# Attention and two feed-forward stages on one core: eight one-bank PSUM tiles in place of four two-bank tiles, and a new table of steps

## The chip, the core and the metric

The kernel runs on one core of a Trainium2 chip. The metric is the device time of one execution in microseconds (us). The engines are named as the profile names them: PE (TensorE, the matrix engine), PEld (its weight loads), DVE (VectorE), ACT (ScalarE), POOL (GpSimd) and SP (SyncE, which issues the DMAs here).

## What is computed

Causal attention over 2 x 12 heads of 448 tokens and 64 dimensions, whose output (896 tokens x 768) goes through two feed-forward stages. Only the attention is touched by the change.

```python
scores = scale * np.matmul(q, k.transpose(0, 1, 3, 2))
scores = np.where(mask, -1000000000.0, scores)
scores = scores - np.max(scores, axis=-1, keepdims=True)
attn = np.exp(scores)
attn = attn / (np.sum(attn, axis=-1, keepdims=True) + 1e-09)
x = np.matmul(attn, v)                      # heads laid side by side: 896 x 768
h = x @ w_in                                # 768 x 2048
x = (h * (1.0 / (1.0 + np.exp(-h)))) @ w_out
# then a second stage: 768 x 1024, softmax, product, layer norm, 1024 x 768
```

## The kernel before

The 24 heads are done as 12 pairs, two heads at a time on the two halves of the 128 partitions. A pair's 448 queries are cut into seven units u of 64 queries; unit u needs only the first 64(u+1) keys. For a pair p the steps are these, with the names that the table of steps uses:

- **Sa, Sb** (line 164): scores of units 6, 4, 2, 0 and of units 5, 3, 1, by PE into PSUM.
- **m p.u** (line 170): DVE reads a unit's scores out of PSUM, adds the mask, writes them to the buffer e in SBUF and leaves the row's extreme in st.
- **e p.u** (line 175): ACT takes the exponential in place and sums the row. **r p** (lines 180, 181): DVE adds 1e-9 to the seven sums and takes reciprocals.
- **n p.u** (line 188 on POOL, marked G in the table; line 186 on ACT, marked A): the unit is multiplied by its reciprocals.
- **T p.0, T p.1** (line 202): PE transposes the pair's 16 blocks of 64 queries x 128 keys, for each head, into PSUM, 16 instructions a step.
- **x p.0 to x p.3** (line 216 on ACT, line 214 on DVE, marked V): the transposed weights are copied to the SBUF buffer aT.
- **P p** (line 229): PE multiplies them with the values. **h p** (line 238) and **l p** (line 243) take the result out of PSUM as a rounded part and a rest.
- **g 0 to g 3**: four half blocks of nine matmuls each of the first feed-forward product (lines 395 to 397), put among the last pairs; the weights for them are converted by w, ca, sh (line 276), sl (line 264), rh (line 271), sp, wl, which DVE, ACT and POOL do beside the attention.

Nothing is scheduled by itself here: the text ORDER is read from left to right, and each engine's instructions stand in that order in its queue. An engine works its queue strictly in order, so a step that waits holds all that stands behind it on the same engine. The number after a slash names the PSUM slot that a step writes. Before, there are four slots of two banks each (`SLOTS = 4`). A slot is one tile, so a step that takes it over waits until everything in both banks has been read: T 4.1 into slot 3, which holds the scores Sa of pair 6, waits for the maxima of units 6, 4, 2 and 0 of pair 6. P takes a slot of two banks and fills one. The copies x p.0 to x p.3 are cut by key block, for both heads together, and are 896, 128, 640 and 384 columns wide.

The pieces that set this:

```python
def slot(n):
    return (pss if n == SLOTS - 1 else psx).tile([128, 2, 512], F32, name=f"x{n}", tag=f"x{n}")
PARTS_T = [[(0, range(UNITS)), (3, range(6, UNITS))], [(1, range(2, UNITS)), (2, range(4, UNITS))]]
```

Behind the attention follow only matmuls of the feed-forward stages on PE, with the conversion of weights, activations and evictions on the other engines. The attention and the four g steps end where the ninth matmul of g 3 gives way to the main loop of line 395.

## Time and profile before

| | us |
|---|---|
| median of 3 runs | 397.04 (396.93 to 397.53) |
| the profiled execution: its own time | 397.12 |
| the profiled execution: span of the core | 395.2 |
| PE busy in the span | 387.5 |
| DVE, ACT, POOL busy in the span | 290.3, 279.7, 188.6 |
| granted TensorE clock | 1.00 of full speed in all slices |

The span is the time from the first to the last instruction of the core; the 1.9 us between it and the execution's own time lie around it. Busy times overlap, since the engines work side by side. A row of the timeline gives the start, the length and the count of a run of equal instructions; a bracket at its end tells how long the engine stood idle before it and what ended that.

### The profile page before, as it was taken

What the parts mean: (1) busy time and instruction counts of PE and PEld (TensorE: products, weight loads), DVE (VectorE), ACT (ScalarE), POOL (GpSimd) and SP (SyncE); (2) the same over time, 40 slices, a digit from 0 to 9 for tenths busy, and PEclk for the clock granted to TensorE, in tenths of its full rate; (3) what the DMA queues carried; (4) which work ended last, traced back from release to release, by engine and by line L of the source; (5) the groups of instructions that cost most, each with busy time, mean ns of one, the idle gap of its engine ahead of it and who ended that gap; (6) DMA issues with size and microseconds to landing.
All of it is one profiled execution on the core that took longest, in us unless ns stands there. A gap on an engine that the chain in (4) does not pass through costs nothing.

```text
span 395.2 us, 8157 instructions
## 1 busy us (share of the span) xinstructions
PE 387.5 (98%) x2914; PEld 364.0 (92%) x2914; DVE 290.3 (73%) x681; ACT 279.7 (71%) x655; POOL 188.6 (48%) x236
## 2 busy tenths in 40 slices
...
GB/s 235 399 213 139 101 7 77 81 127 153 127 116 119 121 119 120 117 124 202 89 152 120 191 179 230 238 245 224 14 80 121 98 62 2 20 41 41 41 81 60
DMA packets 20152, 49.68 MB, mean 126 GB/s; under 512 B 2320, under 2 KB 4880, under 8 KB 20112
## 3 DMA queue, kind: packets, MB, share of 16 engines
...
q8 instruction: 23, 0.38, 0.4%
...
## 4 chain that ended last, share of the span: by engine, by line
PE 92%; DVE 4%; ACT 3%; issue 0%
PE h L397 8%; PE h L396 8%; PE h L395 8%; PE h L824 5%; PE h L825 5%; PE h L826 5%; PE ps L904 5%; PE h L555 4%; PE h L557 4%; PE h L556 4%; PE ps L906 4%; PE ps L905 4%; PE x L229 4%; PE x L164 3%; ACT e L175 3%; PE x L202 2%
## 5 line engine op out<-in xcount | busy, mean ns | idle before, releaser
L259 ACT ACTIVATE wr<-wr 128x384 f32<-128x384 f32 x92 | 54.3, 591 | 10.4 <-DMA wr<-w_in 10.2
L396 PE MATMUL h<-l,wh 128*128 128x448 f32 x174 | 61.3, 352 | 0.0
L395 PE MATMUL h<-h,wh 128*128 128x448 f32 x174 | 61.3, 352 | 0.0
L397 PE MATMUL h<-h,wl 128*128 128x448 f32 x174 | 61.3, 352 | 0.0
L289 DVE SCALAR_TENSOR_TENSOR pw<-wr,pw 128x384 uint32<-128x384 uint32 x78 | 43.5, 557 | 13.3 <-ACT pw L285 13.2
L188 POOL TENSOR_TENSOR e<-e,st 128x64 f32<-128x64 f32 (+6 forms) x76 | 45.5, 633 | 11.4 <-DVE st L170 6.9
L414 POOL TENSOR_TENSOR gl<-sg,gh 128x448 fp32r<-128x448 f32 x29 | 32.7, 1145 | 36.9 <-ACT sg L412 36.9
L175 ACT ACTIVATE e<-e,st 128x256 f32<-128x256 f32 (+6 forms) x84 | 41.8, 507 | 4.2 <-DVE st L170 4.1
L326 DVE TENSOR_TENSOR wl<-pw,wh 128x384 fp32r<-128x384 f32 x30 | 16.7, 557 | 32.5 <-ACT wh L322 31.8
L322 ACT ACTIVATE wh<-pw 128x384 fp32r<-128x384 f32 x30 | 14.8, 493 | 36.1 <-PE h L396 27.5
L170 DVE CUSTOM_DVE_ANT_0 e<-x,mask 128x448 f32<-128x448 f32 (+6 forms) x84 | 30.5, 414 | 5.4 <-PE x L164 5.4
L858 POOL TENSOR_TENSOR s<-s,mhalf 128x1 f32<-128x1 f32 x7 | 4.2, 594 | 61.3 <-DVE s L857 61.3
L326 POOL TENSOR_TENSOR wl<-wx,wh 128x384 fp32r<-128x384 f32 x21 | 21.2, 1008 | 25.5 <-ACT wh L322 25.4
L395 PEld LDWEIGHTS h<-h,wh 128*128 128x128 f32 x174 | 32.9, 189 | 0.1
L397 PEld LDWEIGHTS h<-h,wl 128*128 128x128 f32 x174 | 32.9, 189 | 0.0
L396 PEld LDWEIGHTS h<-l,wh 128*128 128x128 f32 x174 | 32.9, 189 | 0.0
L824 PE MATMUL h<-w3h,h 128*128 128x512 f32 x84 | 31.9, 380 | 0.0
L825 PE MATMUL h<-w3l,h 128*128 128x512 f32 x84 | 31.9, 379 | 0.0
L826 PE MATMUL h<-w3h,l 128*128 128x512 f32 x84 | 31.8, 379 | 0.0
L555 PE MATMUL h<-gh,wh 128*128 128x448 f32 x90 | 31.7, 352 | 0.0
L557 PE MATMUL h<-gh,wl 128*128 128x448 f32 x90 | 31.7, 352 | 0.0
L556 PE MATMUL h<-gl,wh 128*128 128x448 f32 x90 | 31.7, 352 | 0.0
...
## 6 DMA issues: line engine op xcount, KB each, us to landing
...
gain<-gl_in SPq DMA_DIRECT2D x1, 4.0 KB, 3.9
```

Of the source, the lines that this page charges most:

```text
L175: nc.scalar.activation(ep(p, u), ep(p, u), AF.Exp, bias=st[p % 4][:, u:u + 1], scale=-1.0, accum_out=st[p % 4][:, 8 + u:9 + u])
L188: eng.tensor_tensor(ep(p, u), ep(p, u), r.to_broadcast([128, wide(u)]), ALU.mult)
L259: nc.scalar.activation(high, high, AF.Copy, scale=DOWN)
L395: nc.tensor.matmul(ps[:, :S], wh, rh, start=turn == 0 and k % NB == 0, stop=False)
L396: nc.tensor.matmul(ps[:, :S], wh, rl, start=False, stop=False)
L397: nc.tensor.matmul(ps[:, :S], wl, rh, start=False, stop=turn == 1 and k % NB == NB - 1)
L555: nc.tensor.matmul(ps[:, :S], wh, rh, start=f == CF[0], stop=False)
L556: nc.tensor.matmul(ps[:, :S], wh, rl, start=False, stop=False)
L557: nc.tensor.matmul(ps[:, :S], wl, rh, start=False, stop=f == CF[-1])
L824: nc.tensor.matmul(ps[:, n], yh[k][:, at], wh, start=k == 0, stop=False)
L825: nc.tensor.matmul(ps[:, n], yh[k][:, at], wl, start=False, stop=False)
L826: nc.tensor.matmul(ps[:, n], yl[k][:, at], wh, start=False, stop=k == KD - 1)
```

## The change

PSUM is cut into eight tiles of one bank (`SLOTS = 8`, 512 columns). A step names one bank a digit: Sa and Sb take two, T takes two (one a head), P takes one. Each bank is given back when its own contents have been read. The transposed weights lie in aT by head and block (head, 16 blocks of 64 columns, key blocks in the order 0, 3, 1, 2), and the copies x p.0 to x p.3 become four equal ones of 512 columns: first and second half of the blocks, each for head 0 and head 1. The second product reads them at the places that `FROM_T` gives. No matmul and no maximum is added or taken away. The table of steps is new as a whole. Net of all, ACT has five instructions less and POOL five more: the norms 4.4, 8.0, 8.1, 10.4 and 10.1 and the conversion ca 3 go from ACT to POOL, in pair 11 ACT does four norms in place of three; h 11 goes from ACT to DVE; ACT does 25 of the 48 copies x in place of 24, DVE 23.

```diff
--- before.py
+++ after.py
@@ -48,7 +48,7 @@
 MASKED = -1.0e9 / SCALE
 
 
-SLOTS = 4
+SLOTS = 8
 UNITS = S // C
 SWAPPED = (1, 2, 3, 4)
 BANKS = ((6, 0), (4, 2), (5,), (3, 1))
@@ -59,27 +59,28 @@
 
 
 ORDER = """
-q1 q2 q3 v0 Sx0/0 v1 v2 m0.1 Sy0 m0.0 e0.1 e0.0 Sz0 m0.3 m0.2 e0.3 Sw0 m0.5 e0.2 e0.5 Sa1/3 m0.4 q4 m0.6 w0 e0.4 Sb1/1
...
+q1 q2 q3 v0 Sx0/0 v1 v2 m0.0 Sy0 m0.1 e0.1 e0.0 Sz0 m0.2 Sw0 m0.3 e0.2 m0.5 e0.3 e0.5 Sa1/45 m0.4 q4 m0.6 w0 e0.4
...
 """
 
 
@@ -147,7 +148,7 @@
         scs = {}
 
         def slot(n):
-            return (pss if n == SLOTS - 1 else psx).tile([128, 2, 512], F32, name=f"x{n}", tag=f"x{n}")
+            return (pss if n >= SLOTS - 2 else psx).tile([128, 512], F32, name=f"x{n}", tag=f"x{n}")
 
         sa, sb, sc = {}, {}, {}
 
@@ -156,7 +157,7 @@
             banks, swapped = (BANKS, SWAPPED) if p else (FIRST_BANKS, FIRST)
             for u in us:
                 n = next(n for n, bank in enumerate(banks) if u in bank)
-                t = (sa, sb, sc)[n // 2][p][:, n % 2]
+                t = (sa, sb, sc)[n // 2][p][n % 2]
                 o = sum(wide(v) for v in banks[n][:banks[n].index(u)])
                 scs[p, u] = t = t[:, o:o + wide(u)]
                 for j in range(2):
@@ -191,25 +192,23 @@
 
         aT, trs = {}, {}
 
-        PARTS_T = [[(0, range(UNITS)), (3, range(6, UNITS))], [(1, range(2, UNITS)), (2, range(4, UNITS))]]
-        HALVES = [[(u, kb) for kb, us in part for u in us] for part in PARTS_T]
+        BLOCKS_T = [(u, kb) for kb in (0, 3, 1, 2) for u in range(2 * kb, UNITS)]
+        FROM_T = [BLOCKS_T.index((2 * kb, kb)) for kb in range(NKB)]
 
         def transp(p, g, n):
-            t = slot(n).rearrange("k h (n q) -> k h n q", q=C)
-            for m, (u, kb) in enumerate(HALVES[g]):
+            for h in range(2):
+                trs[p, 2 * g + h] = slot(int(n[h]))
+            for m, (u, kb) in enumerate(BLOCKS_T[8 * g:8 * g + 8]):
                 for h in range(2):
-                    r = slice(C * h, C * h + C)
-                    nc.tensor.transpose(t[:, h, m], es[p % EB][r, AT[u] + kb], ident[r, r])
-            trs[p, g] = t
+                    r, t = slice(C * h, C * h + C), trs[p, 2 * g + h]
+                    nc.tensor.transpose(t[:, C * m:C * m + C], es[p % EB][r, AT[u] + kb], ident[r, r])
 
         def evict(p, n, eng):
             if p not in aT:
-                aT[p] = att.tile([128, NKB, 2, S], F32, name="aT", tag=f"aT{p % AB}", bufs=1)
-            a = aT[p]
-            kb, us = PARTS_T[n // 2][n % 2]
-            m = n % 2 and len(HALVES[n // 2]) - len(us)
-            src = trs[p, n // 2][:, :, m:m + len(us)]
-            dst = a[:, kb, :, C * us[0]:].rearrange("k h (n q) -> k h n q", q=C)
+                aT[p] = att.tile([128, 2, 16, C], F32, name="aT", tag=f"aT{p % AB}", bufs=1)
+            g, h = divmod(n, 2)
+            dst = aT[p][:, h, 8 * g:8 * g + 8]
+            src = trs[p, n].rearrange("k (n q) -> k n q", q=C)
             if eng is nc.vector:
                 eng.tensor_copy(dst, src)
             else:
@@ -218,15 +217,16 @@
         pvs = {}
 
         def pv(p, n):
-            t = pvs[p] = slot(n)[:, 0]
+            t = pvs[p] = slot(n)
             v = vs[p]
             for z in range(NKB):
                 for lo, hi, swap in RUNS if p else FIRST_RUNS:
-                    sl = slice(C * max(lo, 2 * z), C * hi)
+                    lo = max(lo, 2 * z)
+                    sl, at = slice(C * lo, C * hi), FROM_T[z] + lo - 2 * z
                     for h in range(2):
                         j = h ^ swap
                         if sl.start < sl.stop:
-                            nc.tensor.matmul(t[64 * j:64 * j + 64, sl], v[:, j, z], aT[p][:, z, h, sl],
+                            nc.tensor.matmul(t[64 * j:64 * j + 64, sl], v[:, j, z], aT[p][:, h, at:at + hi - lo],
                                              start=z == lo == 0, stop=z == NKB - 1, skip_group_check=True)
 
         def pv_hi(p, eng):
@@ -435,7 +435,7 @@
             rounded(th[4][:, k], tl[4][:, k], sgs[FB[k], 0], nc.gpsimd)
 
         nc.vector.memset(xl[0][:, :S].bitcast(F32), 0.0)
-        wp = slot(SLOTS - 1)[:, 0]
+        wp = slot(SLOTS - 1)
 
         def warm(count):
             for _ in range(count):
@@ -467,19 +467,19 @@
             gemm1(f, half, 0, turn)
 
         def scores_to(tiles, p, n, us):
-            if n is not None:
-                tiles[p] = slot(n)
+            if n:
+                tiles[p] = [slot(int(b)) for b in n]
             scores(p, us)
 
         emit = {
-            "Sx": lambda p, n, u, e: scores_to(sa, p, n, (0, 1)), "Sy": lambda p, n, u, e: scores_to(sb, p, 1, (2, 3)),
-            "Sz": lambda p, n, u, e: scores_to(sc, p, 2, (5,)), "Sw": lambda p, n, u, e: scores(p, (6, 4)),
+            "Sx": lambda p, n, u, e: scores_to(sa, p, "01", (0, 1)), "Sy": lambda p, n, u, e: scores_to(sb, p, "2", (2, 3)),
+            "Sz": lambda p, n, u, e: scores_to(sc, p, "4", (5,)), "Sw": lambda p, n, u, e: scores(p, (6, 4)),
             "Sa": lambda p, n, u, e: scores_to(sa, p, n, (6, 4, 2, 0)), "Sb": lambda p, n, u, e: scores_to(sb, p, n, (5, 3, 1)),
             "q": lambda p, n, u, e: load_pair(p), "v": lambda p, n, u, e: load_v(p),
             "w": lambda m, n, u, e: load_w(*order[m]),
             "m": lambda p, n, u, e: maxes(p, u), "e": lambda p, n, u, e: exps(p, u), "r": lambda p, n, u, e: recip(p),
             "n": lambda p, n, u, e: norm(p, u, e), "T": lambda p, n, u, e: transp(p, u, n),
-            "x": lambda p, n, u, e: evict(p, u, e), "P": lambda p, n, u, e: pv(p, n),
+            "x": lambda p, n, u, e: evict(p, u, e), "P": lambda p, n, u, e: pv(p, int(n)),
             "h": lambda p, n, u, e: pv_hi(p, e), "l": lambda p, n, u, e: pv_lo(p),
             "ca": lambda m, n, u, e: conv_a(1, m, e), "sh": lambda m, n, u, e: shift_w(1, m),
             "sl": lambda m, n, u, e: sign_low(1, m, fresh(xs)), "rh": lambda m, n, u, e: rest_high(1, m),
@@ -493,7 +493,7 @@
             step, _, part = step.rstrip("AVG").partition(".")
             name = step.rstrip("0123456789")
             u = int(part) if part else None
-            emit[name](int(step[len(name):]), int(n) if n else None, u, e)
+            emit[name](int(step[len(name):]), n, u, e)
         fed[0] = EARLY
         gm = gm[0]
         psx.release()
```

The first place is PE's queue at pair 2 (buffer e2; x with a digit is the PSUM slot or bank). Before, from the transposes T 2.0 on:

```order
L202 MATMUL x3_476<-ident_70,e2_99 128x64 x16
L164 MATMUL x1_496<-qk_211 64x448 x2
L164 MATMUL x1_496<-qk_211 64x320 x2
L164 MATMUL x1_496<-qk_211 64x192 x2
L164 MATMUL x1_496<-qk_211 64x64 x2
L202 MATMUL x2_514<-ident_70,e2_99 128x64 x16
L164 MATMUL x0_534<-qk_211 64x384 x2
L164 MATMUL x0_534<-qk_211 64x256 x2
L164 MATMUL x0_534<-qk_211 64x128 x2
L229 MATMUL x3_550<-aT_509,v32_159 64x64 x2
```

With the change, from the last two of the 32 transposes of the same pair on:

```order
L204 MATMUL x7_513<-ident_70,e2_99 128x64
L204 MATMUL x5_514<-ident_70,e2_99 128x64
L165 MATMUL x6_533<-qk_214 64x448 x2
L165 MATMUL x0_534<-qk_214 64x320 x2
L165 MATMUL x0_534<-qk_214 64x192 x2
L165 MATMUL x6_533<-qk_214 64x64 x2
L165 MATMUL x4_550<-qk_214 64x384 x2
L165 MATMUL x3_551<-qk_214 64x256 x2
L165 MATMUL x3_551<-qk_214 64x128 x2
L229 MATMUL x5_564<-aT_544,v32_160 64x64 x2
```

Both halves of the transposes now stand together ahead of all seven units of scores (of pair 5), where before scores stood between them.

The second place is DVE's queue ahead of the transposes of pair 4, with the maxima of pair 6 (buffer e2; x3 and x0 are slots before, x6, x7 and x0 banks now). Before, T 4.1 goes into slot 3 and needs all of x3_623 read:

```order
L271 SCALAR_TENSOR_TENSOR wx_505<-wr_196,wx_505 128x384
L214 COPY aT_619<-x1_601 128x2x192
L214 COPY aT_619<-x1_601 128x2x320
L170 ISA e2_99,st2_103<-x3_623,mask_96 128x448
L170 ISA e2_99,st2_103<-x0_636,mask_96 128x128
L170 ISA e2_99,st2_103<-x3_623,mask_96 128x320
L180 TENSOR_SCALAR st1_102<-st1_102 128x7
L181 RECIPROCAL st1_102<-st1_102 128x7
```

With the change T 4.1 goes into banks 4 and 6 and needs, of these, x6_653 alone:

```order
L213 COPY aT_638<-x1_619 128x512
L213 COPY aT_638<-x4_620 128x512
L271 SCALAR_TENSOR_TENSOR wx_510<-wr_198,wx_510 128x384
L171 ISA e2_99,st2_103<-x6_653,mask_96 128x64
L171 ISA e2_99,st2_103<-x6_653,mask_96 128x448
L171 ISA e2_99,st2_103<-x7_654,mask_96 128x320
L181 TENSOR_SCALAR st1_102<-st1_102 128x7
L182 RECIPROCAL st1_102<-st1_102 128x7
```

The two copies moved ahead of line 271, and the two maxima that T 4.1 waits for stand first; before, the last one that it waits for (128x192 of x3_623) stood behind the reciprocals and two further maxima.

The third place is ACT's queue at the copies of pairs 1 and 2 (aT_414 and aT_509 before; aT_425 and aT_544 now; e3 belongs to pair 3, e0 to pair 4, h1 is the taking-out of pair 1). Before:

```order
L216 ACTIVATE aT_414<-x0_374 128x896
L216 ACTIVATE aT_414<-x0_374 128x2x64
L175 ACTIVATE e3_100,st3_104<-e3_100,st3_104 128x192
L175 ACTIVATE e3_100,st3_104<-e3_100,st3_104 128x384
L175 ACTIVATE e3_100,st3_104<-e3_100,st3_104 128x128
L175 ACTIVATE e3_100,st3_104<-e3_100,st3_104 128x448
```

With the change:

```order
L215 ACTIVATE aT_425<-x1_384 128x512
L176 ACTIVATE e3_100,st3_104<-e3_100,st3_104 128x128
L176 ACTIVATE e3_100,st3_104<-e3_100,st3_104 128x448
L215 ACTIVATE aT_425<-x7_385 128x512
L176 ACTIVATE e3_100,st3_104<-e3_100,st3_104 128x384
L176 ACTIVATE e3_100,st3_104<-e3_100,st3_104 128x320
L176 ACTIVATE e0_97,st0_101<-e0_97,st0_101 128x192
L176 ACTIVATE e0_97,st0_101<-e0_97,st0_101 128x320
L176 ACTIVATE e0_97,st0_101<-e0_97,st0_101 128x128
L238 ACTIVATE h1_74<-x1_458 128x448
L176 ACTIVATE e0_97,st0_101<-e0_97,st0_101 128x64
L176 ACTIVATE e0_97,st0_101<-e0_97,st0_101 128x384
```

Two exponentials of pair 3 now stand between the two copies of pair 1; behind the last row follow the two copies of pair 2.

## Rows read from the trace of the kernel before

**Rows 1.** The page: busy time of each engine; the chain that ended last, by engine

```profile
PE 387.5 (98%) x2914; PEld 364.0 (92%) x2914; DVE 290.3 (73%) x681; ACT 279.7 (71%) x655; POOL 188.6 (48%) x236
...
PE 92%; DVE 4%; ACT 3%; issue 0%
```

**Rows 2.** Busy time by stretch: length, then PE, PEld, DVE, ACT, POOL

```profile
40.00:45.00 5.00, 5.00 (x98) 4.01 (x100) 4.85 (x21) 5.00 (x19) 4.49 (x10) 1.00 0.44 161
73.00:395.00 322.00, 318.45 (x1773) 308.88 (x1771) 228.15 (x440) 213.97 (x438) 133.09 (x126) 1.00 0.38 117
```

**Rows 3.** Timeline of PE, 14 to 36 us: start, length, what, idle before it

```profile
16.67 1.99 PE L229 MATMUL x<-aT,v 128*64 128x256 f32 x36 [0.79 <-ACT aT L216]
18.59 1.21 PE L202 MATMUL x<-ident,e 64*128 64x64 f32 x32
19.73 1.74 PE L164 MATMUL x<-qk 64*64 64x448 f32 x28
21.40 1.98 PE L229 MATMUL x<-aT,v 128*64 128x64 f32 x32
23.31 0.71 PE L202 MATMUL x<-ident,e 64*128 64x64 f32 x16
...
24.98 0.71 PE L202 MATMUL x<-ident,e 64*128 64x64 f32 x16
...
26.43 1.98 PE L229 MATMUL x<-aT,v 128*64 128x64 f32 x32
28.34 1.50 PE L202 MATMUL x<-ident,e 64*128 64x64 f32 x32
29.77 1.74 PE L164 MATMUL x<-qk 64*64 64x448 f32 x28
...
33.41 0.71 PE L202 MATMUL x<-ident,e 64*128 64x64 f32 x16
34.58 0.72 PE L202 MATMUL x<-ident,e 64*128 64x64 f32 x16 [0.46 <-DVE st L170]
35.22 1.09 PE L164 MATMUL x<-qk 64*64 64x448 f32 x12
```

**Rows 4.** The same timeline: the first matmul of g 3

```profile
72.48 0.46 PE L395 MATMUL ps<-h,wh 128*128 128x448 f32 x1
```

**Rows 5.** Timeline of DVE, 29 to 35 us

```profile
29.78 1.23 DVE L271 SCALAR_TENSOR_TENSOR wx<-wr,wx 128x384 uint32<-128x384 uint32 x1
...
32.13 0.61 DVE L170 CUSTOM_DVE_ANT_0 e<-x,mask 128x448 f32<-128x448 f32 x1
...
34.07 0.35 DVE L170 CUSTOM_DVE_ANT_0 e<-x,mask 128x192 f32<-128x192 f32 x1
```

**Rows 6.** Timeline of ACT, 19 to 22 us

```profile
19.57 1.07 ACT L216 ACTIVATE aT<-x 128x896 f32<-128x896 f32 x2
...
21.57 0.39 ACT L175 ACTIVATE e<-e,st 128x128 f32<-128x128 f32 x1
...
21.95 0.66 ACT L175 ACTIVATE e<-e,st 128x448 f32<-128x448 f32 x1
```

**Rows 7.** Groups by line and shape, 0 to 75 us: busy us, mean ns

```profile
L216 ACT ACTIVATE aT<-x 128x896 f32<-128x896 f32 x11 | 10.0, 912 | 0.0
L214 DVE COPY aT<-x 128x640 f32<-128x640 f32 x11 | 9.0, 817 | 0.0
...
L214 DVE COPY aT<-x 128x384 f32<-128x384 f32 x11 | 6.0, 547 | 0.0
...
L271 DVE SCALAR_TENSOR_TENSOR wx<-wr,wx 128x384 uint32<-128x384 uint32 x5 | 3.8, 762 | 0.0
...
L216 ACT ACTIVATE aT<-x 128x128 f32<-128x128 f32 x11 | 3.0, 272 | 1.0 <-PE x L202 1.0
```

**Rows 8.** The same view: norms on POOL, and the conversion ca

```profile
L188 POOL TENSOR_TENSOR e<-e,st 128x320 f32<-128x320 f32 x10 | 7.2, 719 | 0.9 <-DVE st L181 0.9
...
L188 POOL TENSOR_TENSOR e<-e,st 128x128 f32<-128x128 f32 x10 | 4.3, 430 | 0.4 <-DVE st L181 0.4
...
L257 POOL TENSOR_TENSOR wr<-wr,down 128x384 f32<-128x384 f32 x4 | 3.3, 827 | 0.0
```

More of the change, by code (lines that the diff above doesn't have):

```diff
@@ L67 @@
-x1.3V n2.4G e3.5 m4.6 n2.6G P1/0 e3.1 q8 m4.1 m4.4 e3.6 v7 n2.3G m4.2 e4.1 m4.0 r3 ca0G e4.2 m4.3 T2.0/3 e4.4 m4.5
-n3.2G Sa5/1 sl0 h1A n3.1G x2.1A n3.5G e4.0 l1 T2.1/2 x2.0A n3.0G m5.0 Sb5/0 m5.2 n3.4G e5.0 x2.2V e4.6 n3.3G q9 x2.3V
-P2/3 e4.3 n3.6G v8 m5.5 e4.5 m5.3 ca1G e5.5 m5.4 T3.0/2 r4 h2A ca2G m5.6 e5.4 l2 T3.1/1 n4.5G x3.1A x3.0A m5.1 Sa6/3
-rh0 n4.2G e5.6 n4.0G Sb6/0 x3.3V n4.1G n4.4A x3.2V n4.6G e5.1 P3/2 q10 e5.3 m6.6 n4.3G v9 e5.2 m6.1 m6.4 e6.1 r5 e6.4
-T4.0/1 m6.3 n5.5G h3A m6.0 m6.2 x4.0A m6.5 T4.1/3 n5.2G l3 n5.1G Sa7/0 x4.1A e6.2 n5.4G x4.2V e6.3 Sb7/1 n5.0G x4.3V
@@ L82 @@
-P10/2 rh3 x11.2A x11.3A w7 sp3 P11/1 h10A wl3 l10 g3 h11A l11
+q1 q2 q3 v0 Sx0/0 v1 v2 m0.0 Sy0 m0.1 e0.1 e0.0 Sz0 m0.2 Sw0 m0.3 e0.2 m0.5 e0.3 e0.5 Sa1/45 m0.4 q4 m0.6 w0 e0.4
+Sb1/67 v3 m1.4 e0.6 m1.6 q5 e1.4 Sa2/23 r0 w1 m1.2 e1.6 n0.4G v4 m1.5 Sb2/01 e1.2 m1.1 n0.2G m2.6 e1.1 q6 n0.5G Sb3/56
+e1.5 m1.0 m2.0 w2 m1.3 n0.3G Sa3/42 e1.0 v5 m2.1 m2.3 e2.0 n0.1G m2.4 e1.3 n0.0G m3.2 q7 n0.6G e2.3 r1 w3 e2.4 m3.4 v6
+n1.4G m2.2 T0.0/71 e2.1 m3.6 e2.2 T0.1/23 n1.5G m2.5 x0.1A x0.3V n1.0G x0.0A n1.1G e2.5 x0.2V n1.3G P0/0 e2.6 m3.3
@@ new lines @@
+n1.6G m3.5 e3.3 r2 n1.2G e3.2 m3.1 m3.0 n2.4G T1.0/17 h0A sh0 e3.0 T1.1/32 n2.1G l0 x1.0A n2.5G Sa4/56 e3.1 x1.3V e3.6
+n2.2G x1.2V Sb4/40 n2.0G x1.1A ca0G m4.6 e3.5 q8 P1/1 m4.3 n2.3G v7 m4.2 e3.4 m4.0 n2.6G m4.4 e4.2 m4.1 e4.4 r3 m4.5
+T2.1/23 n3.3G e4.1 sl0 h1A T2.0/75 n3.6G e4.0 Sa5/60 e4.5 x2.3V n3.1G x2.1A x2.2V n3.0G Sb5/43 n3.5G x2.0A m5.0 l1
+e5.0 n3.4G P2/5 q9 e4.3 m5.5 v8 ca1G e4.6 m5.1 m5.4 m5.3 e5.1 n3.2G m5.2 e5.3 ca2G r4 T3.0/27 h2A m5.6 T3.1/14 n4.1G
+x3.1A l2 n4.5G Sb6/30 x3.0A x3.2V e5.6 Sa6/67 n4.6G x3.3V e5.2 rh0 P3/5 n4.4G e5.4 q10 e5.5 v9 n4.3G m6.0 m6.6 n4.0G
```

27 lines of the change are left out of this document (13 added, 14 removed).

## The prediction

> **What bounds the kernel now.** I read the page first: PE is busy 98% of the span and holds 92% of the chain that ended last [rows 1]. The stretches split this. From 73 us on PE has work 318.45 of 322 us, while DVE, ACT and POOL have idle time; no part of that stretch is touched by the change. So a microsecond by which the attention ends sooner or later on PE should reach the end almost whole. In the attention three further engines are close to full: from 40 to 45 us ACT is busy 5.00 of 5, DVE 4.85, POOL 4.49 [rows 2]. There PE leads by little, and a queue that is reordered can push it in either direction.
>
> The timeline of PE shows what is to be had. An undisturbed pair is the one that starts at 18.59: transposes to 19.73 (1.14), scores to 21.40 (1.67), values to 23.31 (1.91), together 4.72 us [rows 3]. The attention ends with g 3 starting at 72.48 [rows 4]. Whatever PE loses against the undisturbed pair between 16.67 and 72.48 is the change's to gain; matmuls themselves are the same before and after, so none of them gets shorter.
>
> **The change part by part.**
>
> *Copies.* ACT did one copy of 896 columns (912 ns) and one of 128 (272), together 1184; DVE did 640 (817) and 384 (547), together 1364 [rows 7]. A line through ACT's two gives 592 for 512 columns, through DVE's two 682: twice that is 1184 and 1364. Cost and gain nil. The layout of aT moves the same columns; I put nothing for it, since PE reads runs of the same lengths.
>
> *Start.* PE begins the first product with the values at 16.67, released by ACT's copy [rows 3]. In ACT's queue 19 exponentials stand ahead of that copy in both kernels, the same pieces of pairs 0 to 2, and then two copies of equal sum. I put no gain; a gain can't be over the 0.79 us of that wait.
>
> *Pair 2 of the transposes.* Scores stand between its halves. From 23.31 to the values at 26.43 PE takes 3.12 us; the undisturbed pair does the same work in 2.81 (18.59 to 21.40) [rows 3]. The new table keeps the halves together: **-0.31**.
>
> *Pair 3.* From 28.34 to 29.77 the transposes take 1.43 in place of 1.14 [rows 3]. Before, their second half needs the maxima of Sa of pair 5, whose last stands behind a reciprocal step that waits for ACT. Now it takes banks that the table frees earlier (the maximum of unit 5 and a copy of pair 1's result): **-0.29**.
>
> *Pair 4.* From 33.41 to 35.22 the transposes take 1.81, 0.46 of it a plain wait on DVE [rows 3]. DVE had just done a long line 271 (29.78, 1.23 us), two copies and the maxima down to the one at 34.07 that T 4.1 needs [rows 5]. With the change T 4.1 needs only the maximum of unit 6 of those, which came out at 32.13 + 0.61 = 32.74 even in the old order [rows 5], well before PE is there: **-0.67**.
>
> Together -1.27. After 35 us PE has hardly a gap in the old trace, so the finer banks have nothing more to release there.
>
> *New wait at pair 1.* ACT's first copy of pair 1 starts at 19.57 in the old trace, and the two take 1.07 in a row [rows 6] where they are 1184 ns by themselves [rows 7]: pieces overlap by 0.11, and two copies hold the queue 0.96, one of the new ones 0.48. In the new queue two exponentials stand between the copies. First copy, so 20.05; pieces of 128 and 448 columns, 0.39 and 0.66 [rows 6], so 21.10; second copy 0.59, done at 21.69. The products of pair 1 were due at 21.40 [rows 3], and their second matmul reads the other head, that is the second copy: **+0.30**.
>
> *New wait at pair 2.* ACT goes on from 21.10 with half a pair of copies (0.48), exponentials of 384, 320, 192, 320, 128, 64 and 384 columns (on the line through 0.39 and 0.66 [rows 6]: 0.60, 0.55, 0.44, 0.55, 0.39, 0.34, 0.60, sum 3.47), the taking-out of pair 1 (about 0.45, estimated as a copy of 448 between the two of [rows 7], less the 0.1 by which pieces overlap) and the two copies of pair 2 (0.48 and 0.59). That ends at 26.6. PE comes to these products 1.91 + 1.14 + 1.67 after 21.70, at 26.42: **+0.20**.
>
> Bounds for the two together: nothing, if ACT's queue runs ahead by half a microsecond elsewhere, and 1.0, if each doubles as an exponential slips in late. I keep the middle, 0.50.
>
> *SP.* The loads q, v and w keep their order on SP, and each waits only for the release of its own buffer; nothing for them.
>
> *Late pairs.* ACT loses five instructions, POOL gains five. POOL's extra: two norms of 320 columns (2 x 719), two of 128 (2 x 430), one of 64 (under 430), and the conversion (827): about 3.4 us over eight pairs [rows 8]. POOL had 0.51 us in five idle [rows 2]; spread over pairs 4 to 10, and with three g steps in between that give every queue time, I cost it at nothing. What covers it is that lead; without it rival 3 holds. The norms taken from ACT are worth nothing either, as PE doesn't wait for ACT there.
>
> *Line 271 and POOL.* Line 271 took 1.23 us at 29.78 against a mean of 762 ns for its five here [rows 5, 7]. The Trainium skill (SBUF — State Buffer, "SBUF: two separate sides") says that DVE instructions with two inputs from SBUF and POOL share a port pair under an exclusive lock, and the loser is blocked for the other's whole instruction; by that rule, POOL's added instructions speak against this change, and one such block would take the sum to about nil (rival 4). I don't add a term: the sum is by the trace, in which the change adds no instruction of line 271.
>
> Sum: -1.27 + 0.50 = -0.77. The profiled execution took 397.12 us, so 396.35; it lies 0.08 above the median of the runs, 397.04, which gives 396.27. **I predict 396.3 us.** About 0.2%, 0.8 us, is what a measurement of this kernel can tell from no change: under 396.25 is faster, over 397.83 slower.
>
> **The rivals.**
>
> 1. *ACT takes back what the banks give* (chance 0.21). Per pair ACT has seven exponentials (on the line of [rows 6], 3.49), copies 0.96 and the taking-out 0.45: 4.90 us against PE's 4.72. If its lead is used up, every pair's products wait for the last copy, some 0.18 a pair over pairs 3 to 7, 0.90 in all: -0.77 + 0.90 gives 397.2, no change. For it: ACT busy 5.00 of 5 [rows 2]. Against it: the old trace has PE wait for ACT only once after the start.
>
> 2. *No new wait, and an earlier start* (chance 0.20). If ACT's lead swallows the two waits, -1.27 stays, and if the last norm of pair 0 and the copies come sooner, a part of the 0.79: 395.8 without the latter, 395.3 with half of 0.79 on top.
>
> 3. *POOL becomes the bound* (chance 0.07), the case on the other side. Place: transposes of pairs 4, 8 and 10, which need all seven norms. Price: 0.72, 0.73 and 1.15 us of added norms [rows 8], less 0.5 idle a pair, is 1.1; the conversion adds 0.83 ahead of pair 6. It decides once POOL ends a pair's seventh norm after PE has come to that pair's transposes. -0.77 + 1.93: 398.2.
>
> 4. *The lock* (chance 0.04). If one added POOL piece of 0.72 [rows 8] holds up DVE ahead of a maximum that PE needs, 0.72 comes back: 397.0. That is what the rule of the Trainium skill (SBUF — State Buffer, "SBUF: two separate sides") would do here.
>
> **How the numbers follow.** My forecast has a chance of 0.48, and with the bounds of its own waits it lies between 395.9 and 396.8; a little under half of it falls below 396.25. Faster: 0.22 from it and all 0.20 of rival 2, 0.42. Slower: rival 3 and 0.01 of rival 1, should ACT fall behind further, 0.08. The same: what is left, 0.50. A range from 395.6 to 397.2 leaves out the far end of rival 2 and rival 3, less than 2 in 10.
>
> **What would show it.** In PE's timeline after: the transposes of pairs 2, 3 and 4 take 1.14 us each in one run of 32, with no wait on DVE near 34 us; small waits on ACT ahead of the products of pairs 1 and 2, of 0.2 to 0.3 us; the first products at 16.7; g 3's nine matmuls start near 71.7; and from there the same PE work to the end. Wrong would be: waits on POOL at the transposes of pairs 4, 8 or 10; waits on ACT at every pair; a start of the first products that moved by more than 0.3 us; or an attention that ends sooner while the end doesn't.

## The result, and the profile after

The changed kernel takes 399.9 us (median of 6 runs, 398.28 to 400.33), the kernel before 396.99 (median of 6, 396.89 to 397.53): 2.9 us slower by the medians; the ratio, with its 95% interval, is 1.0064 [1.0045, 1.0083]. I had predicted 396.3 and given this side 0.08. The profiled execution of the changed kernel took 400.17 us.

The page of the changed kernel, busy time of each engine and the chain that ended last, to set beside [rows 1]:

```profile
PE 390.5 (98%) x2914; PEld 366.6 (92%) x2914; DVE 291.8 (73%) x681; ACT 278.1 (70%) x650; POOL 192.3 (48%) x241
...
PE 89%; DVE 6%; POOL 2%; DMA 1%; ACT 1%; issue 0%; SPq 0%; DVEq 0%
```

The five instructions went from ACT to POOL as the table says, and PE is busy 3.0 us longer with the same 2914 matmuls. DVE and POOL now hold 8% of the chain.

Busy time by stretch of the changed kernel (length, then PE, PEld, DVE, ACT, POOL, then PE's granted clock, the DMA share and GB/s), the answers to [rows 2] and three stretches more:

```profile
8.00:17.31 9.31, 7.45 (x118) 5.13 (x116) 9.02 (x46) 8.78 (x33) 6.14 (x12) 1.00 1.03 399
17.31:20.72 3.41, 3.41 (x36) 3.03 (x36) 2.80 (x13) 2.12 (x8) 3.41 (x7) 0.50 1.03 398
20.72:62.00 41.28, 41.00 (x754) 33.83 (x751) 39.57 (x152) 39.77 (x135) 37.35 (x61) 1.00 0.32 104
40.00:45.00 5.00, 5.00 (x98) 4.10 (x96) 4.97 (x19) 4.75 (x17) 4.57 (x8) 1.00 0.78 274
76.10:398.10 322.00, 318.45 (x1773) 308.88 (x1771) 228.01 (x441) 213.23 (x437) 133.04 (x126) 1.00 0.38 117
```

The last row equals the second of [rows 2] in every PE figure, 3.1 us later: nothing is lost behind the attention. The second row is new: for 3.41 us PE ran at a granted clock of 0.50, that is at 1.2 GHz in place of 2.4, and its 36 matmuls there are just the first products P 0.

The timeline of PE in the changed kernel, its answers to [rows 3] and [rows 4] (start, length, what, idle before it):

```profile
17.31 3.61 PE L229 MATMUL x<-aT,v 128*64 128x256 f32 x36 [0.84 <-ACT aT L215]
20.86 1.21 PE L204 MATMUL x<-ident,e 64*128 64x64 f32 x32
...
23.67 2.21 PE L229 MATMUL x<-aT,v 128*64 128x64 f32 x32
25.80 1.21 PE L204 MATMUL x<-ident,e 64*128 64x64 f32 x32
26.95 1.74 PE L165 MATMUL x<-qk 64*64 64x448 f32 x28
28.72 1.98 PE L229 MATMUL x<-aT,v 128*64 128x64 f32 x32
30.63 1.43 PE L204 MATMUL x<-ident,e 64*128 64x64 f32 x32
...
35.63 1.55 PE L204 MATMUL x<-ident,e 64*128 64x64 f32 x32
...
67.79 1.15 PE L204 MATMUL x<-ident,e 64*128 64x64 f32 x30 [0.29 <-POOL e L189]
...
75.58 0.46 PE L395 MATMUL ps<-h,wh 128*128 128x448 f32 x1
```

g 3 starts at 75.58 in place of 72.48: 3.10 us, all of the loss. P 0 starts at 17.31 (16.67 before) and ends 3.55 us later (1.92 before). Transposes come in one piece now, but the pieces of 1.43 and 1.55 us still hold gaps, and a new wait on POOL stands at pair 10.

From the starts in this timeline the loss can be split by stretch. T p, S p and P p stand here for all transposes, score products and value products of pair p; a length runs from one start to the next. The same table holds one profiled execution of each of the experiments below ("fall": the clock stood at 0.50 during P 0; "stall": a DVE step was held for over 4 us, see e6), in us:

| kernel | T 0 to P 0 | P 0 | to P 4 | P 4 to P 6 | P 6 to g 3 | P 0 to g 3 |
|---|---|---|---|---|---|---|
| before | 2.50 | 1.92 | 18.31 | 9.66 | 25.92 | 55.81 |
| changed (fall) | 3.34 | 3.55 | 17.92 | 9.88 | 26.92 | 58.27 |
| e1 old table, eight banks | 2.83 | 1.92 | 18.29 | 9.96 | 26.01 | 56.18 |
| e2 m2.2 ahead of r1 | 2.82 | 2.08 | 18.72 | 9.88 | 26.91 | 57.59 |
| e3 PE filled | 3.26 | 2.02 | 18.60 | 9.88 | 26.90 | 57.40 |
| e4 before, P 0 late (fall) | 3.09 | 3.41 | 18.05 | 9.72 | 25.92 | 57.10 |
| e5 norms on ACT | 3.35 | 1.92 | 17.95 | 10.09 | 26.95 | 56.91 |
| e6 changed, no addition (stall) | 3.09 | 1.92 | 22.31 | 9.67 | 26.73 | 60.63 |
| e7 old table mended | 2.78 | 1.93 | 18.03 | 10.23 | 25.90 | 56.09 |
| e8 e7, no addition (fall, stall) | 2.95 | 3.37 | 17.95 | 15.55 | 25.85 | 62.72 |
| e9 old start, then new | 2.72 | 1.96 | 18.70 | 9.87 | 27.10 | 57.63 |
| e10 new, old from P 6 (fall) | 3.34 | 3.39 | 18.04 | 9.88 | 26.49 | 57.80 |
| e11 before, more on ACT | 2.27 | 2.01 | 18.67 | 10.71 | 25.92 | 57.31 |
| e12 before, more on DVE | 2.28 | 1.92 | 18.49 | 11.19 | 25.93 | 57.53 |

For the changed kernel against before: P 0 starts 0.64 late, lasts 1.63 longer, then -0.39, +0.22 and +1.00. Together 3.10. One execution differs from another by some tenths in such a stretch: before, e11 and e12 have the same order up to P 4, and took 18.31, 18.67 and 18.49 us from the end of P 0 to there.

What ACT waited for from 8 to 62 us in the changed kernel (total, times, longest):

```profile
ACT h L238 <- PE x L229: 1.8, 2, 1.5
ACT e L176 <- DVE st L171: 0.6, 2, 0.4
ACT wh L322 <- DVE wx L271: 0.6, 1, 0.6
ACT aT L215 <- PE x L204: 0.2, 1, 0.2
```

And the same stretch by busy time, first the kernel before, then the changed one:

```profile
8.00:62.00 54.00, 51.45 (x934) 41.41 (x927) 52.51 (x216) 53.91 (x188) 46.24 (x75) 1.00 0.50 178
```

```profile
8.00:62.00 54.00, 51.86 (x902) 41.99 (x901) 51.39 (x209) 50.67 (x175) 46.90 (x77) 0.97 0.49 174
```

This is the view that I should have asked for. Before, ACT is busy 53.91 of 54 us: it does not rest from 8 us on until the last pairs. In the changed kernel it rests 3.33 us and has done 13 instructions fewer by 62 us; 1.5 us of the rest is one wait for the slow P 0. DVE (52.51 before) is nearly as full.

Why P 0 is late shows on POOL, then on DVE, then on ACT. POOL, the changed kernel, 13.8 to 14.8 us:

```profile
13.87 0.93 POOL L189 TENSOR_TENSOR e<-e,st 128x448 f32<-128x448 f32 x1
```

DVE, 13.9 to 15.7 us:

```profile
13.92 0.91 DVE L181 TENSOR_SCALAR st<-st 128x7 f32<-128x7 f32 x1
14.86 0.20 DVE L182 RECIPROCAL st<-st 128x7 f32<-128x7 f32 x1
14.98 0.44 DVE L171 CUSTOM_DVE_ANT_0 e<-x,mask 128x320 f32<-128x320 f32 x1
15.35 0.35 DVE L171 CUSTOM_DVE_ANT_0 e<-x,mask 128x192 f32<-128x192 f32 x1
```

ACT, the same time:

```profile
14.83 0.39 ACT L176 ACTIVATE e<-e,st 128x128 f32<-128x128 f32 x1
15.74 0.46 ACT L176 ACTIVATE e<-e,st 128x192 f32<-128x192 f32 x1 [0.43 <-DVE st L171]
16.20 1.06 ACT L215 ACTIVATE aT<-x 128x512 f32<-128x512 f32 x2
```

The addition of r 1 works on seven columns. The same addition for pair 2 took 0.17 us at 18.66; this one took 0.91, up to the end of the norm of 448 columns that POOL had begun at 13.87. The new table has m 2.2 behind r 1 and e 2.2 ahead of the copies x 0.1 and x 0.0, so ACT waited 0.43 us with the copies that P 0 needs behind it. The Trainium skill (SBUF — State Buffer, "SBUF: two separate sides") says that POOL and a DVE instruction in a 2-port performance mode, or with two inputs from SBUF, lock a shared port pair against each other: whichever starts first has it for its whole instruction, and the other is blocked. This row agrees with that (0.91 us for work of 0.17); the addition has one input, and in which mode it ran no run here shows.

### The profile page after: what moved, and what is told of

It reads as the page before. It is cut to its first block, busy times and chain, and to the rows that moved or that the text cites. A ratio compares the mean times of both kernels' runs of the same rounds, so it can differ in the third digit from the quotient of the medians.

```text
span 398.4 us, 8159 instructions
## 1 busy us (share of the span) xinstructions
PE 390.5 (98%) x2914; PEld 366.6 (92%) x2914; DVE 291.8 (73%) x681; ACT 278.1 (70%) x650; POOL 192.3 (48%) x241
## 4 chain that ended last, share of the span: by engine, by line
PE 89%; DVE 6%; POOL 2%; DMA 1%; ACT 1%; issue 0%; SPq 0%; DVEq 0%
PE h L397 8%; PE h L396 8%; PE h L395 8%; PE h L824 5%; PE h L825 5%; PE h L826 5%; PE ps L904 5%; PE h L555 4%; PE h L557 4%; PE h L556 4%; PE ps L906 4%; PE ps L905 4%; DVE e L171 3%; PE x L229 3%; PE x L165 3%; POOL e L189 2%
## 5 line engine op out<-in xcount | busy, mean ns | idle before, releaser
L259 ACT ACTIVATE wr<-wr 128x384 f32<-128x384 f32 x91 | 53.8, 592 | 10.5 <-DMA wr<-w_in 10.4
L189 POOL TENSOR_TENSOR e<-e,st 128x448 f32<-128x448 f32 (+6 forms) x80 | 48.6, 641 | 11.2 <-ACT e L176 7.0
L176 ACT ACTIVATE e<-e,st 128x128 f32<-128x128 f32 (+6 forms) x84 | 41.7, 503 | 4.8 <-DVE st L171 4.6
L326 DVE TENSOR_TENSOR wl<-pw,wh 128x384 fp32r<-128x384 f32 x30 | 16.7, 557 | 32.9 <-ACT wh L322 32.3
L322 ACT ACTIVATE wh<-pw 128x384 fp32r<-128x384 f32 x30 | 14.8, 493 | 36.7 <-PE h L396 29.6
L171 DVE CUSTOM_DVE_ANT_0 e<-x,mask 128x384 f32<-128x384 f32 (+6 forms) x84 | 30.7, 413 | 5.5 <-PE x L165 5.2
```

The costliest lines, as they stand in the source:

```text
L189: eng.tensor_tensor(ep(p, u), ep(p, u), r.to_broadcast([128, wide(u)]), ALU.mult)
L259: nc.scalar.activation(high, high, AF.Copy, scale=DOWN)
```

## The experiments

Theories: **A**, the start (r 1 held, P 0 late, the clock) makes most of the loss and POOL's added norms the rest; **C**, which came later, ACT and DVE bound the attention, and any order that makes them rest costs that rest; **B**, the rival to A in each part: waits taken away come back elsewhere.

**e1: the eight banks with the old table.** Old slot n became banks 2n and 2n+1; layout, copies and code as changed.

```diff
-... T3.0/27 h2A m5.6 T3.1/14 n4.1G x3.1A l2 n4.5G Sb6/30 ...
+... T3.0/45 r4 h2A ca2G m5.6 e5.4 l2 T3.1/23 n4.5G x3.1A ...
```

> The eight banks, the new layout of aT and the four equal copies, but the old table of steps, each old slot written as its two banks. If the structure itself is slow (equal copies, layout, one-bank tiles), this is near 399.9 us. If the new table is what costs, it is near the kernel before: 396.7 to 397.1, a little under it, since a bank is given back sooner; the granted clock stays at 1.00 throughout.

396.99 us (median of 10), ratio 0.9992 [0.9982, 1.0001]. So banks, layout and copies are free, and all of the loss lies in the table. PE's rows at pairs 3 and 4 of this kernel:

```profile
28.00 0.71 PE L204 MATMUL x<-ident,e 64*128 64x64 f32 x16
29.49 0.71 PE L204 MATMUL x<-ident,e 64*128 64x64 f32 x16 [0.78 <-DVE st L171]
30.13 1.74 PE L165 MATMUL x<-qk 64*64 64x448 f32 x28
...
33.71 1.21 PE L204 MATMUL x<-ident,e 64*128 64x64 f32 x32
```

T 3 took 2.13 and T 4 1.14 us; before it was 1.43 and 1.81 [rows 3]. A wait had moved from pair 4 to pair 3, and the sum is the same, 3.27 against 3.24. I took that as a first hint that these waits are conserved. But DVE's rows give another reading: the addition of r 4 stands ahead of the maximum that T 3 waited for, and it was held until a conversion ended that POOL had begun at 27.84.

```profile
27.81 0.88 DVE L181 TENSOR_SCALAR st<-st 128x7 f32<-128x7 f32 x1
```

In the four profiled executions with the old order and no fall the waits go with such holds almost one for one. The addition of r 4 took 0.17, 0.17, 0.59 and 0.88 us in before, e11, e12 and e1, and T 3 1.43, 1.42, 1.85 and 2.13. Line 271 behind it took 1.23 [rows 5], 1.23, 0.57 and 0.57 us, and T 4 1.81, 1.81, 1.15 and 1.14. So the wait stood where POOL held DVE.

**e2: m2.2 ahead of r1** in the changed kernel.

```diff
-... e2.3 r1 w3 e2.4 m3.4 v6 n1.4G m2.2 T0.0/71 ...
+... e2.3 m2.2 r1 w3 e2.4 m3.4 v6 n1.4G T0.0/71 ...
```

> The changed kernel with one step moved: the maximum of unit 2 of pair 2 stands ahead of the reciprocals of pair 1 on DVE. In the changed kernel those reciprocals took 0.91 us beside a norm on POOL, and the maximum, its exponential and ACT's copies of pair 0 stood behind them. If that is the cause of the late start, the first value products start at 16.7 in place of 17.31. Whether the clock then still falls to half shows whether the 0.6 us decide it: 397.7 us if it stays at 1.00 (0.6 and 1.6 back), 399.3 if it falls all the same.

399.32 us, ratio 1.0053 [1.0037, 1.0069]. T 0 to P 0 shrank by 0.52 us to 2.82, so r 1's hold was the cause of that wait. P 0 itself started at 17.24 and not at 16.7, because ACT was late already near 9 us, ahead of the moved step: from its exponential of 320 columns there to the copies it needed 6.85 us, as before, against 7.40 in the changed kernel. In the profiled execution the clock did not fall. It was still slow: 57.59 us from P 0 to g 3 against 55.81. So the time that I had expected with a fall (399.3) came, by luck, with a profiled execution that had none, and the start is not the main part.

**e3: PE filled**, two matmuls of zeros ahead of each half of T 0 and of P 0 in the changed kernel.

```diff
+            for _ in range(2 if p == 0 else 0):
+                nc.tensor.matmul(t[:, :S], xl[0][:, :128], xl[0][:, :S], start=True, stop=True)
```

> The changed kernel with six matmuls of zeros, two ahead of each half of pair 0's transposes and two ahead of its value products, in banks that are overwritten afterwards; nothing else is moved. If PE's sparse work ahead of 17.3 us lets the clock fall, it stays at 1.00 and 1.6 us come back: 398.3 us, with the first products still at 17.3 to 17.4. If the slow products have another cause (the new layout, the copies), they take 3.5 us as before and the time is 399.9 or slightly above.

399.52 us, ratio 1.0062 [1.0045, 1.0079]. The profiled execution had no fall and lost 1.59 us between P 0 and g 3; with e2 that gives +1.6 to +1.8 us for the order without the clock. It is the fastest of the four, though (398.46, the others 399.47 to 399.72, with a mean clock of 0.998 to 0.999), so whether the filling keeps the clock up is not shown.

**e4: the kernel before with P 0 late**, e 2.5 put ahead of the copies.

```diff
-... x0.1A n1.0G m3.5 x0.0A n1.5G x0.2V e3.4 n1.2G x0.3V P0/2 e2.5 ...
+... e2.5 x0.1A n1.0G m3.5 x0.0A n1.5G x0.2V e3.4 n1.2G x0.3V P0/2 ...
```

> The kernel before with one exponential of pair 2 (384 columns) moved ahead of ACT's copies of pair 0, so that its first value products start 0.6 us later, near 17.3. If the late start alone makes the clock fall, the products take 3.5 us in place of 1.9 and the time is near 399.2 us. If something of the changed kernel is needed, it loses 0.6 at most: 397.6.

399.11 us, ratio 1.0040 [1.0020, 1.0061]. The clock fell here too. Busy time by stretch:

```profile
18.30:21.72 3.42, 3.42 (x40) 3.10 (x38) 1.45 (x7) 1.55 (x7) 3.02 (x6) 0.50 1.02 398
```

P 0 started at 18.05 (3.09 us behind T 0 in place of 2.50; T 0 itself began 0.79 later) and took 3.41 us; from P 0 to g 3 1.29 us were lost. So the fall needs neither the changed kernel's banks nor its order: a late P 0 in the old order brought it, with a mean clock of 0.994 or 0.995 in all four executions. That a late P 0 always brings it is not so, as e5 shows. ACT was busy 1.55 of the 3.42 us: a slow P 0 makes ACT and DVE wait as well.

**e5: norms back on ACT**, in the changed kernel.

```diff
-... n4.4G ... ca3G ... n8.1G ... n8.0G ... n10.1G ... n10.4G ...
+... n4.4A ... ca3A ... n8.1A ... n8.0A ... n10.1A ... n10.4A ...
```

> The changed kernel with six pieces of work put from POOL back on ACT: the norms n4.4, n8.0, n8.1, n10.1, n10.4 and the conversion ca3. Theory A (POOL ends the waits ahead of the transposes of pairs 9 and 10, through the work that the new table gave it): T9 and T10 fall from 1.43 and 1.65 us to 1.14 to 1.25, T4 from 1.48 by up to 0.3, P0 stays late and its clock may fall; the time goes from 399.9 to about 399.1. Theory B (the table's waits lie in its order, whichever engine does the work): ACT ends the same waits instead, T9 and T10 keep 1.4 to 1.7 us, and the time stays 399.6 to 400.2.

400.07 us (median of 10), ratio 1.0043 [1.0025, 1.0061]. The ten fall into two groups: four with a mean clock of 1.00 took 397.95 to 398.88 us (median 398.66), six with 0.991 to 0.996 took 400.05 to 400.66 (median 400.35). The profiled one (398.88) is of the first, with P 0 3.35 us behind T 0 and no fall. So the median, which B had right, depends on how many executions fell, and the rows must decide. T 9 and T 10 fell to 1.14 us each, as A said, but P 6 to g 3 took 26.95 us (26.92 in the changed kernel). The wait stood at pair 11:

```profile
69.25 1.21 PE L204 MATMUL x<-ident,e 64*128 64x64 f32 x32 [0.54 <-POOL e L189]
```

DVE's rows say why: r 11 had to wait for ACT, which was now late with the exponentials.

```profile
66.55 0.52 DVE L181 TENSOR_SCALAR st<-st 128x7 f32<-128x7 f32 x1 [1.25 <-ACT e L176]
```

For the late pairs B is right: with the norms on ACT the same time is lost at pair 11, so POOL's added norms alone were not the cause.

**e6: the changed kernel without the addition of 1e-9** to the row sums (r is the reciprocal alone; that part of the computation is left out).

```diff
-            nc.vector.tensor_scalar(t[:, 8:8 + UNITS], t[:, 8:8 + UNITS], 1e-9, None, ALU.add)
```

> The changed kernel with the addition of 1e-9 to the row sums left out, so that r is the reciprocal alone. Theory A (r1's addition, held for the length of POOL's norm, makes the first products late, and the late start lets TensorE's clock fall): m2.2 starts 0.7 to 1.0 us earlier against T0, P0 starts 2.4 to 2.9 us after T0 instead of 3.3, the clock stays at 1.0 through P0, which takes 1.92 us; T9 and T10 keep their waits (1.43 and 1.65, less what an earlier r gives them); the time comes to 397.6 to 398.6. Theory B (the first products are late for another reason, the order of ACT's steps): P0 stays over 3.2 us behind T0, and the time is 399.2 or more.

400.97 us (median of 10, from 396.69 to 402.62), ratio 1.0061 [1.0025, 1.0097]. P 0 came 3.09 us behind T 0, without a fall: nothing held r 1, but ACT's queue had been late since 9 us, so the copies started at 16.15 us, as in the changed kernel (16.20). Neither expectation had that number. From ACT's exponential of 320 columns near 9 us to the copies it was 6.85 us again, as in e2, so this wait was gone here too. And a new stall made the spread. DVE and POOL of the profiled execution:

```profile
18.91 5.09 DVE L275 TENSOR_SCALAR wr<-wr 128x384 uint32<-128x384 uint32 x1
```

```profile
15.64 5.90 POOL L188 TENSOR_TENSOR e<-e,st 128x384 f32<-128x384 f32 x11
21.49 0.83 POOL L256 TENSOR_TENSOR wr<-wr,down 128x384 f32<-128x384 f32 x1
22.28 1.51 POOL L188 TENSOR_TENSOR e<-e,st 128x256 f32<-128x256 f32 x2
```

The step sh 0 was held from 18.91 until POOL's queue ran dry at 23.79, over eight POOL instructions. PE stood idle for 2.54 us for it, and P 1 ran at half clock. The median therefore tests nothing. But the three fastest executions took 396.69, 397.55 and 397.62 us (mean clock 0.999 to 1.00), no more than the kernel before on the same chip (397.64): without the additions the new order need not be slower. No trace of such an execution was kept, so how much of the loss hangs on holds of r stays open.

**e7: the old table mended**, in eight banks: T 2.1 in banks 1 and 5 right behind T 2.0, its DVE copies ahead of m 5.2, m 5.6 ahead of r 4, and the conversions ca 1 and ca 2 a pair later; some later tiles lie in other banks for it.

```diff
-... T2.0/67 e4.4 m4.5 n3.2G Sa5/23 sl0 h1A n3.1G x2.1A n3.5G e4.0 l1 T2.1/45 ...
+... T2.0/67 T2.1/15 e4.4 m4.5 n3.2G Sa5/23 sl0 h1A n3.1G x2.1A n3.5G e4.0 l1 ...
```

> The eight banks with the old table, but for: pair 2's transposes in one piece (T2.1 in banks 1 and 5, free by then), its two DVE copies ahead of m5.2, m5.6 ahead of r4, and the conversions ca1 and ca2 on POOL one pair later. Theory A (with the order kept, single banks give back what the prediction said: the two extra switches of pair 2 and the wait in pair 3's transposes): T2 1.14, S5 1.67, T3 at most 1.4 (2.13 with the old table alone), T4 at most 1.3; the time is 396.0 to 396.5. Theory B (each wait taken away comes back at the next transposes, on POOL or ACT): T3 and T4 together keep 3.2 us, and the time is 396.8 to 397.1.

397.14 us (median of 10) beside 397.64 for the kernel before on the same chip, ratio 0.9984 [0.9971, 0.9997]: the lowest ratio here, but by less than the 0.2% that I had set as telling a change from none. The trace goes with B. T 2 took 1.14 us, S 5 1.75 and T 4 1.39, but T 3 took 1.72 and T 5 1.64 in place of 1.14. From P 0 to g 3 it is 56.09 us against 55.81, so the small gain in time isn't explained by this execution.

```profile
29.27 0.71 PE L204 MATMUL x<-ident,e 64*128 64x64 f32 x16 [0.29 <-DVE st L181]
...
39.55 0.71 PE L204 MATMUL x<-ident,e 64*128 64x64 f32 x15 [0.23 <-DVE st L171]
```

Ahead of T 5's wait POOL again held an addition, that of r 6: 0.84 us at 38.05.

**e8: e7 without the addition of 1e-9** (left out as in e6).

> The kernel before this one in the list, with the addition of 1e-9 to the row sums left out too. Theory A (r is held by POOL's norms at some pairs, 0.4 to 0.9 us each, and what follows is late): another 0.2 to 0.6 us less, 395.5 to 396.2, P0 no later than 2.6 us behind T0. Theory B (r's hold is hidden in this order): the same time as the kernel before this one within 0.2 us.

Three of the eleven executions took 403.4 to 403.8 us. One of them is the profiled one, and it has the stall of e6: sh 1, the same instruction for another block of weights, took 4.07 us from 40.18, until POOL's queue ran dry. The other eight have a median of 397.2 us and a ratio of 0.9988 [0.9973, 1.0003]. No gain over e7 can be told, so in the old order the holds of r cost nothing that shows.

**e9: the old order up to P 0, the new one for the rest.**

```diff
+[old table up to] x0.3V P0/4
 m3.6 e2.5 n1.3G e2.6 m3.3 n1.6G e3.3 r2 e3.2 n2.4G T1.0/75 ... h11V l11
```

> The changed kernel with the old table's order up to the first products P0, and the new table's order for all that is left; banks given out anew. Theory A (most of what was lost lies at the start: P0 0.64 us late and 1.62 us at half clock): P0 starts 2.5 to 2.9 us behind T0, the clock stays at 1.0, and the rest waits as in the changed kernel (from P0 to g3 57.2 to 57.6 us, 55.8 before): 398.2 to 398.8, about 1.3 us over the kernel before. Theory C (ACT bounds the attention, and every rest that the new order gives it is lost): the same start, but the later waits change with ACT's rests; ACT rests at least 1 us in all between 8 and 62 us where it rested 0.1 before. Rival: the new order behind P0 is no worse once its start is right: 397.2 or less.

398.75 us, ratio 1.0032 [1.0019, 1.0045]; no execution shows the fall's mean clock of 0.994 to 0.996. P 0 came 2.72 us behind T 0. From P 0 to g 3 57.63 us, 1.82 more than before, as in e2 and e3; ACT rested 1.87 of 54 us. So by the times 1.3 us of the 2.9 remain with the old start, and they come from the order behind it.

**e10: the new order up to P 6, then the old one.**

```diff
 [new table up to] x6.3V P6/7
+e8.2 n7.1G e8.3 n7.0G n7.3G m9.0 m9.6 e8.5 ... x11.2A x11.3A w7 sp3 P11/5 h10A wl3 l10 g3 h11A l11
```

> The changed kernel up to P6, and from there the old table's order (with n8.0, n8.1, n10.1, n10.4 and ca3 on ACT and h11 on ACT, as before). Theory A and C: the waits at T9, T10 and the first products of pair 9 (0.29 + 0.51 + 0.09 us) and the score products of pair 11 (0.18) go, as the order there is the old one: g3 comes 0.7 to 1.1 us earlier against P6, 398.9 to 399.3 with the fall of the clock, 397.3 to 397.7 without. Rival (pair 11 is late because the first half left ACT behind): the waits come at T10 and T11 instead, with the same sum, and the time stays within 0.3 us of 399.9.

399.99 us, ratio 1.0058 [1.0037, 1.0078]. P 6 to g 3 took 26.49 us, between the two tables' 25.92 and 26.92: 0.43 of the 1.00 goes with the late order. The other 0.57 is brought along, since waits came earlier, mostly at the scores behind T 7 (1.71 in place of 1.46) and at T 8 (1.33 in place of 1.14). Both expectations were half right.

**e11 and e12: the kernel before with more work on one engine**, meant for near 45 us, where PE has no gap (they ran from 41 us on): two copies of 448 columns on ACT behind e 7.3, or two additions on DVE behind x 5.3, into rows that nothing reads.

```diff
+            "z": lambda m, n, u, e: nc.scalar.activation(spare_rows, mask, AF.Copy),
+            "z": lambda m, n, u, e: nc.vector.tensor_tensor(spare_rows, mask, mask, ALU.add),
```

> The kernel before with two more copies of 448 columns on ACT, into rows that nothing reads, behind e7.3 (near 45 us, where TensorE has no waits and ACT no rest); by the copies h of 448 columns 0.54 us each, some 1.1 us in all. Theory C (ACT bounds the attention): the first products of TensorE behind it wait, and g3 is later by 0.9 to 1.1 us: 398.0 to 398.2. Rival (ACT is full only because its queue runs ahead; it has room until pair 11): later by at most 0.3 us, 397.0 to 397.4.

> The kernel before with two more additions of 448 columns on DVE, into rows that nothing reads, behind x5.3 (near 45 us); some 1.1 us in all, by l's 0.6 us each. If DVE is as much the bound as ACT: g3 later by 0.9 to 1.1 us. If ACT alone bounds the attention: later by at most 0.3 us. A hold by POOL's norms would show as a longer duration of the added rows themselves.

Ratios 1.0020 [1.0007, 1.0033] and 1.0023 [1.0013, 1.0034]. First e11, the added rows with the next row on ACT, and PE's transposes of pair 5:

```profile
40.94 1.19 ACT L490 ACTIVATE extra<-mask 128x448 f32<-128x448 f32 x2
42.03 0.44 ACT L176 ACTIVATE e<-e,st 128x192 f32<-128x192 f32 x1
```

```profile
44.65 0.71 PE L203 MATMUL x<-ident,e 64*128 64x64 f32 x16 [0.83 <-DVE st L171]
```

Then e12, the same of DVE and PE:

```profile
41.48 1.57 DVE L490 TENSOR_TENSOR extra<-mask 128x448 f32<-128x448 f32 x2
42.98 0.61 DVE L171 CUSTOM_DVE_ANT_0 e<-x,mask 128x448 f32<-128x448 f32 x1
```

```profile
45.40 0.71 PE L203 MATMUL x<-ident,e 64*128 64x64 f32 x16 [1.16 <-DVE st L171]
```

ACT was held 1.09 us (42.03 - 40.94), and T 5 took 2.19 in place of 1.14: +1.05. DVE was held 1.50 (42.98 - 41.48), and T 5 took 2.62: +1.48. Between P 4 and P 6 the two lost 1.05 and 1.53 against before, and from P 6 to g 3 nothing came back (25.92 and 25.93). So in the old order neither engine has any room at pair 5: what delays either of them reaches PE whole. That is theory C, for both engines, at this one place. In the medians beside the kernel before (397.42) it is less, +0.8 us for e11 and +1.0 for e12, where the trace has 1.48.

## Why the prediction was wrong

The ledger, from the table above: P 0 starts 0.64 us late, and from P 0 to g 3 another 2.46 are lost, to the new order and to the clock's fall. Without a fall the new order lost 1.6 to 1.8 us there in e2, e3 and e9, which leaves 0.7 to 0.9 for the fall. P 0 itself lost 1.63 to it, but ACT and DVE went on meanwhile with what was released, and PE met fewer waits behind it: the stretch to P 4 was 17.92 us with the fall and 18.60 to 18.72 in those three. This split is not settled, for each of these is one execution, and others disagree. e5 had no fall, yet took 17.95 us to P 4 and lost 1.10 in all; e4 lost 1.29 with the fall in the old order; and the two groups of e5's executions are 1.7 us apart. By e4 and these groups the fall costs 1.3 to 1.7 and the new order 0.8 to 1.2.

For theory C speaks that ACT's rest from 8 to 62 us goes with what PE lost from P 0 to g 3 against before, in the profiled executions without fall or added work: 0.33 and 0.28 us in e7, 0.26 and 0.37 in e1, 1.23 and 1.10 in e5, 1.87 and 1.82 in e9, 2.03 and 1.59 in e3, 2.12 and 1.78 in e2. That shows that the two go together, not which comes first.

- **"Pair 2, -0.31; pair 3, -0.29; pair 4, -0.67."** This is the step that failed most. I read each gap of PE as removable by itself, and predicted 1.27 us for the three. Without the fall T 2 and S 5 took 3.10 us in e2 (3.12 before), T 3 1.78 and T 4 1.48: 6.36 us in all, and 6.36 before (3.12 + 1.43 + 1.81). The gain was nil there, -0.06 in e3, 0.35 in e9 and 0.53 in e5. In the profiled execution of the changed kernel it was 0.20, 0.07 and 0.33, with the fall ahead of it. PE's gaps there are where it meets ACT and DVE, which have no room; e11 and e12 show them growing by just what was added, e1 and e7 show them at other pairs with much the same sum, and under e1 they follow DVE's holds. The 0.67 at pair 4 was no fixed cost of the two-bank slot either: it came with a hold of line 271 by POOL, and was gone in e12, which has two-bank slots, where line 271 was not held (the four executions under e1). Which of the later waits are such holds, no run separates.
- **"Start: I put no gain", with P 0 at 16.7.** Wrong by 0.64 us. I counted the exponentials ahead of the copies and found them the same. What differed is what they wait for: e 2.2 for m 2.2, and that stood behind an r 1 held by POOL, 0.43 us on ACT. e2 took this wait away and won 0.52 from T 0 to P 0.
- **The clock.** It has no term and no rival in the prediction. All slices of the old profile stood at 1.00, and I did not ask what would become of that if P 0 came later.
- **"New wait at pair 1, +0.30; at pair 2, +0.20."** Sound in kind: P 1 took 2.13 us in place of 1.91 (+0.22), in e9 2.66 with a plain wait on ACT's copy; P 2 came 1.77 after the start of S 5 in place of 1.67 (+0.10).
- **"Late pairs: costed at nothing."** Wrong by 1.00 us from P 6 to g 3. POOL ends the wait at T 10, as rival 3 had it (the gap of 0.29 us at T 9 shows no releaser), yet e5 shows that POOL's added work alone isn't the cause, and e10 that about half of it comes from the earlier order.
- **The rivals.** Rival 1 was nearest. I took "PE waits for ACT only once" as evidence against it, but ACT without a rest was the evidence for it: 5.00 of 5 us in [rows 2] was the row, read as a lead that PE had. Rival 4's lock struck at the seven columns of r 1, where I had not looked: I had kept to instructions with two inputs, and the addition has one. At line 271 it struck too, 1.21 us at 59.90, and ACT waited 0.6 us for that (the list above).
- **"From 73 us on a microsecond reaches the end almost whole."** Right: 3.10 us at g 3, 3.05 in the profiled times (400.17 and 397.12).

Open: which single steps of the new order behind P 0 make ACT rest. The waits name DVE's m and rh (0.6 us each in 8 to 62) and PE; no run takes them one by one. Open too: how the 2.46 us behind the start split between order and clock, and how much of the order's part are holds of DVE by POOL (e6).
